# Four small moves in a conformer kernel: queries sooner, pending work earlier, copies before a table load, inputs before weights

## The chip, the core and the metric

The kernel runs on one core of one Trainium2 chip. The metric is the device time of one execution in microseconds; for a kernel I quote the median of its executions. "Changed kernel" is the one with all four moves. Span is the time from the first to the last instruction in a profiled execution; it is some 4 us shorter than the device time. The changed kernel and all experiments gave correct results.

## The reference, cut to what matters

```
B, T, D = 2, 4000, 512; F = 2048; K = 3
h = layernorm(x);  x1 = x + 0.5 * silu(h @ w_ff1_a) @ w_ff1_b      # first feed-forward part
h = layernorm(x1); q, k, v = h @ w_q, h @ w_k, h @ w_v
x2 = x1 + softmax(q @ k.T * D**-0.5) @ v @ w_o                      # attention, each batch by itself
h = layernorm(x2) @ w_pw1; h = h[..., :D] * sigmoid(h[..., D:])     # convolution part
h = depthwise conv of 3 taps; normalised over all tokens per channel
x3 = x2 + silu(h) @ w_pw2
x4 = x3 + 0.5 * silu(layernorm(x3) @ w_ff2_a) @ w_ff2_b             # second feed-forward part
return layernorm(x4)
```

All inputs are bf16.

## The kernel before

The 8000 tokens are worked in 16 chunks of up to 508, a chunk in four tiles of 127 rows. TensorE is never meant to stop: every engine gets its instructions in one fixed order, and the order on TensorE mixes work of several stages, so that a group of matmuls whose inputs are late has others in front of it. Weights of queries and keys are folded into one matrix M, so keys are the normalised tokens themselves.

Attention issues, for each of 32 key tiles of a chunk, four matmuls of scores, an exponential on ScalarE, a running sum on VectorE, and then the four matmuls of values of four steps before (they are put on a list of pending work, `lags`). The next chunk's queries are made on the way, in four groups of four matmuls:

```
for g in range(NCK):                                  # 16 chunks
    for kt in range(KT):                              # 32 key tiles
        ...  # scores -> ps; ACT: exp; DVE: acc += P
        def values(...):                              # 4 matmuls into Yb[0..3]
            ...
            if kt == KT - 1: self.finish_queries(g, done)   # copies Yb away: 2 on ACT, 2 on DVE
        self.lags.append(values)
        ...  # pop one pending piece
        if g + 1 < NCK and 7 <= kt < 7 + TPC:
            self.fetch_queries(...)                   # DMA transposes of keys into lnT[slot]
        if g + 1 < NCK and kt in (14, 16, 18, 20):
            self.q_group(..., (kt - 14) // 2)         # 4 matmuls, copy by ACT (even) or DVE (odd)
        ...  # from chunk 1 on: convolution work of earlier chunks as filler
```

In front of it, the first queries:

```
for dc in range(DC):                # DC = 4
    self.q_group(0, 0, dc)
...
self.attention(old, ...)            # old = 2 pieces of the feed-forward part still pending
```

At the end of the convolution part, for the last two chunks, depthwise sums sit in four PSUM banks (Yb) in turn, get statistics from VectorE, and are copied to SBUF by ScalarE. The `act(self.nr1, ...)` is there only to make ScalarE load the table of Silu early:

```
def finish(cc, between=None):
    for t in (last, tail):
        f, copy = self.depthwise(t, cc)   # 3 matmuls into the next Y bank
        f()                               # DVE: statistics
        copies.append(copy)               # ACT: copy out of the bank, to be issued later
        if t == last and between: between()
    self.conv_scale(cc)                   # DVE aggregate, POOL power
...
for jj in range(DC):
    self.conv_b(last, jj)                 # matmuls, ACT: sigmoid
    if jj == DC - 1:
        self.act(self.nr1, self.onef, AF.Silu, ...)
    copy_away()                           # issues all waiting copies
    self.conv_a(last, jj)
    ...
self.swish(0, 0); self.swish(0, 1); copy_away()
...
def between():
    self.conv_shift(DC - 2)               # DVE, needs POOL's power
    self.swish(0, 2)                      # ACT, needs that shift
finish(DC - 1, between)
self.conv_shift(DC - 1); self.swish(0, 3)
```

And the start. Each x tile comes in two transfers, of 112 and 15 rows:

```
for ti in range(TPC):
    self.load_rows(self.XT[ti], ..., ("SP", "ACT" if ti < 2 else "SP"))
for k in range(2):
    self.load_wa(i["w_ff1_a"], k, "ACT")            # 256 KB each
for k in range(self.NWA): ...                       # the other weights, by SP
...
def head(self):
    self.warm(13)                                   # matmuls on zeros
    ...
    for ti in self.ln_tiles(0, 0, None, ("DVE",) * TPC, lag=1):   # layernorm of 4 tiles
        self.transpose_pe(ti, ...)                  # TensorE, copy by ACT (last: DVE)
        if ti: blocks(ti - 1)                       # 16 matmuls, two 256 KB loads as weights
    blocks(TPC - 1)
```

Of the kernel before, what the change touches and what calls it, by code (L numbers as in the profile page):

```python
# [16 lines left out]
TPC = 4  # L17
CHUNK = TPC * TILE
N = B * T
TCB = -(-T // CHUNK)  # L20
NCK = B * TCB
# [6 lines left out]
DC = D // 128  # L28
# [7 lines left out]
def width(c):  # L36

    return CHUNK if c % TCB < TCB - 1 else T - (TCB - 1) * CHUNK
# [214 lines left out]
class Conformer:  # L253
# [604 lines left out]
                                           reads=b_o[lo:hi], writes=[Buf("out")]))  # L858


    def q_group(self, b, qc, dc):

        s, sl = qc % 2, 1 if b or qc else 0
        ps, b_ps = self.sbank()
        W = width(qc)
        out = ps[:, 0:W].rearrange("p (t k) -> p t k", t=TPC)
        lo = self.query_at(qc, 0)[1]
        for cc in range(DC):
            self.mm(out, self.M[:, cc, dc * 128:(dc + 1) * 128], self.lnT[sl][:, :, cc, lo:lo + W // TPC],
                    cc == 0, cc == DC - 1, [self.b_M] + self.b_lnT[sl], b_ps)  # L870
        if dc % 2:
            self.S.op("DVE", lambda e: e.tensor_copy(self.qT[s][:, dc, 0:W], ps[:, 0:W]),  # L872
                      reads=[b_ps], writes=[self.b_qT[s][dc]])
        else:
            self.act(self.qT[s][:, dc, 0:W], ps[:, 0:W], AF.Copy, [b_ps], [self.b_qT[s][dc]])
# [6 lines left out]
        return qc * CHUNK + ti * n - lo, lo  # L882

    def fetch_queries(self, b, qc, ti):
        sl = 1 if b or qc else 0
        src, rd = self.keys_at(b, self.query_at(qc, ti)[0])
        self.transpose(self.lnT[sl][:, ti], src, rd, [self.b_lnT[sl][ti]])

# [35 lines left out]
    def attention(self, old, hook, done):  # L924
        S = self.S
        LAG = 4
        for g in range(NCK):
            b, qc = divmod(g, TCB)
            s, W = qc % 2, width(g)
            if self.any_score:  # L930
                if qc == 0:
                    self.pop(len(self.lags))
                    if b:
                        for kt in range(KT):
                            self.key_tile(1, kt)
                self.row_max(qc)
            for kt in range(KT):
                kc, kj = divmod(kt, TPC)
                ps, b_ps = self.sbank()
                p = self.nxt("Pa", self.NP - 1) if self.any_score else self.nxt("P", self.NP)  # L940
                for cc in range(DC):
                    self.mm(ps[:, 0:W], self.hT[kc][:, kj, cc, :], self.qT[s][:, cc, 0:W],
                            cc == 0, cc == DC - 1 and not self.any_score,
                            [self.b_hT[kc][kj], self.b_qT[s][cc]], b_ps)
                if self.any_score:
                    self.mm(ps[:, 0:W], self.one3, self.m3[:, 0:W], False, True,
                            [self.b_one3] + self.b_m3, b_ps)
                self.act(self.P[p][:, 0:W], ps[:, 0:W], AF.Exp, [b_ps], [self.b_P[p]], scale=SCALE)
                if kt == 0:
                    S.op("DVE", lambda e, p=p: e.tensor_copy(self.acc[s][:, 0:W], self.P[p][:, 0:W]),  # L950
                         reads=[self.b_P[p]], writes=[self.b_acc[s]])
                else:
                    n = REST if kt == KT - 1 else 128
                    acc = self.acc[s][0:n, 0:W]
                    S.op("DVE", lambda e, p=p, n=n, acc=acc: e.tensor_tensor(  # L955
                        out=acc, in0=acc, in1=self.P[p][0:n, 0:W], op=ALU.add),
                        reads=[self.b_P[p], self.b_acc[s]], writes=[self.b_acc[s]])

                if kt == KT - 1:
                    self.split_sums(g)  # L960
                    if g < NCK - 1:
                        self.sums_by_query(s)

                def values(kt=kt, p=p, g=g, W=W):
                    for dc in range(DC):

                        r = slice(dc * REST, (dc + 1) * REST) if kt == KT - 1 else slice(0, 128)
                        self.mm(self.Yb[dc][:, 0:W], self.h[kt][r, dc * 128:(dc + 1) * 128], self.P[p][r, 0:W],
                                kt == 0, kt == KT - 1, [self.b_h[kt], self.b_P[p]], self.b_Y[dc],
                                inc=kt == KT - 1 or dc == DC - 1,  # L970
                                **({"tile_position": (dc * REST, 0)} if kt == KT - 1 else {}))
                    if kt == KT - 1:
                        self.finish_queries(g, done)

                self.lags.append(values)
                if g == 0 and kt < LAG:
                    self.pop({0: old // 2, 1: old - old // 2}.get(kt, 0))
                elif len(self.lags) > LAG:
                    self.pop(1)
                if g + 1 < NCK and 7 <= kt < 7 + TPC:  # L980
                    self.fetch_queries((g + 1) // TCB, (g + 1) % TCB, kt - 7)
                if g + 1 < NCK and kt in (14, 16, 18, 20):
                    self.q_group((g + 1) // TCB, (g + 1) % TCB, (kt - 14) // 2)
                if not self.any_score and TCB - 1 <= g <= TCB:

                    at = (g - TCB + 1) * KT + kt
                    for k in range(KT):
                        if 6 + k * (2 * KT - 12) // KT == at:
                            self.key_tile(1, k)
                hook(g, kt)  # L990
                self.tick()
# [350 lines left out]
    def program(self, any_score):  # L1342
        i = self.i
# [6 lines left out]
        for ti in range(TPC):  # L1350
            self.load_rows(self.XT[ti], self.x_flat[ti * TILE:(ti + 1) * TILE, :], [self.bx[ti]],
                           ("SP", "ACT" if ti < 2 else "SP"))
        for k in range(2):
            self.load_wa(i["w_ff1_a"], k, "ACT")
        for k in range(self.NWA):
            if k > 1:
                self.load_wa(i["w_ff1_a"], k, "SP")
# [35 lines left out]
        old = 0  # L1393
        for c in range(NCK):
            ff1(c, old)
            old = len(self.lags)
        for dc in range(DC):
            self.q_group(0, 0, dc)

        tail = NCK - 2  # L1400
# [74 lines left out]
        copies = []  # L1475

        def finish(cc, between=None):
            for t in (last, tail):
                f, copy = self.depthwise(t, cc)
                f()  # L1480
                copies.append(copy)
                if t == last and between:
                    between()
            self.conv_scale(cc)

        def copy_away():
            while copies:
                copies.pop(0)()

        self.halo_left(last, 0)  # L1490
        for jj in range(DC):
            self.conv_b(last, jj)
            if jj == DC - 1:
                self.act(self.nr1, self.onef, AF.Silu, [self.b_onef], [self.b_nr1])
            copy_away()
            self.conv_a(last, jj)
            if jj > 1:
                self.conv_shift(jj - 2)
            if 0 < jj < DC - 1:
                self.halo_left(last, jj + 1)  # L1500
            if jj:
                finish(jj - 1)
            else:
                self.halo_left(last, 1)
                f, copy = self.depthwise(tail - 1, DC - 1)
                f()
                copies.append(copy)
# [129 lines left out]
```

## Time and profile before

| | |
|---|---|
| Device time, 3 runs | 2042.21 us (2041.98 to 2042.29) |
| Span of the profiled run | 2037.6 us |
| TensorE busy | 2028.8 us |
| Granted TensorE clock | 0.999 |

TensorE is the bound from the start to the end, and the gain of any move that keeps its work is a stall that goes. A stall shows best as a distance between starts of consecutive matmuls: a line of the timeline reads start, duration (both in us), engine, source line, operation, output<-inputs, shape and count, and in brackets the idle time before it with what ended it.

### The profile page before, as it was taken

How to read it: one execution, taken by the hardware profiler on the slowest of the kernel's cores; microseconds unless marked ns; L12 is line 12 of the kernel's file. 1: busy time of each engine (PE TensorE's matmuls, PEld its weight loads, DVE VectorE, ACT ScalarE, POOL GpSimd, SP SyncE). 2: the span in 40 equal slices, each digit the busy share in tenths (PEclk: the TensorE clock that was granted, in tenths of full speed). 3: DMA queues.
4: the chain of work that ended last, by engine and by line, in shares of the span. 5: the costliest groups of instructions: out<-in, count | busy, mean ns of one | idle time of the engine just before them, and what ended most of it. 6: DMA issues, size and time to landing. Idle time of an engine off the chain costs nothing.

```text
span 2037.6 us, 24579 instructions
## 1 busy us (share of the span) xinstructions
PE 2028.8 (100%) x9682; PEld 1030.0 (51%) x9682; DVE 1081.6 (53%) x2187; ACT 743.6 (36%) x1277; POOL 107.6 (5%) x235
## 2 busy tenths in 40 slices
PE   9999999999999999999999999999999999999999
PEld 5555555554444444445444444444455555555555
DVE  4234443334556667666766676667674444434434
ACT  3433333333333333333333333333345443443433
POOL 1000000000000000000000000000011000000000
PEclk9999999999999999999999999999999999999999
DMA  8122245420101111114421111111243111111111
GB/s 189 49 62 62 54 101 124 96 70 8 27 16 26 26 32 26 26 24 94 108 58 23 26 27 34 23 27 26 44 135 93 32 32 42 32 32 42 26 37 38
DMA packets 253121, 104.42 MB, mean 51 GB/s; under 512 B 193412, under 2 KB 252487, under 8 KB 252999
## 3 DMA queue, kind: packets, MB, share of 16 engines
q1 hardware_dynamic: 251793, 102.18, 21.6%
q8 instruction: 78, 1.28, 0.3%
q10 hardware_dynamic: 1206, 0.60, 0.1%
q14 instruction: 44, 0.36, 0.1%
HBM read 33.77 MB, written 23.34 MB: 28 GB/s over the span
## 4 chain that ended last, share of the span: by engine, by line
PE 98%; ACT 1%; DVE 0%; DMA 0%; SPq 0%; issue 0%; ACTq 0%
PE s L512 56%; PE y L512 42%; ACT work L562 0%; DMA xt<-in_x_dram 0%; ACT keys L562 0%; SPq L574 0%; PE y L540 0%; DVE work L559 0%; ACT L562 0%; PE y L527 0%; DVE work L872 0%; DVE work L955 0%; DVE wff L1208 0%; DVE wff L1095 0%; ACT wff L562 0%
## 5 line engine op out<-in xcount | busy, mean ns | idle before, releaser
L562 ACT ACTIVATE work<-s 128x508 bf16<-128x508 f32 (+3 forms) x1060 | 621.6, 587 | 1212.6 <-PE s L512 1208.1
L512 PE MATMUL s<-work,wff 128*128 128x508 bf16 (+4 forms) x2640 | 628.3, 369 | 0.6 <-DVE work L559 0.2
L512 PE MATMUL s<-work,keys 128*128 128x508 bf16 (+1 forms) x2048 | 516.8, 374 | 0.1
L512 PE MATMUL y<-work,keys 128*128 128x508 bf16 (+2 forms) x2048 | 504.2, 373 | 0.4 <-DVE work L559 0.4
L512 PE MATMUL y<-wff,work 128*127 128x512 bf16 (+1 forms) x2000 | 501.4, 378 | 0.0
L955 DVE TENSOR_TENSOR work<-work 128x508 f32<-128x508 f32 (+2 forms) x496 | 334.4, 674 | 283.1 <-ACT work L562 282.1
L512 PEld LDWEIGHTS s<-work,wff 128*128 128x128 bf16 x2640 | 252.5, 98 | 276.9 <-issue 4.7
L512 PEld LDWEIGHTS y<-wff,work 128*127 128x127 bf16 x2000 | 274.4, 137 | 170.8
L512 PEld LDWEIGHTS s<-work,keys 128*128 128x128 bf16 x2048 | 199.5, 98 | 231.9 <-issue 0.6
L512 PEld LDWEIGHTS y<-work,keys 128*128 128x128 bf16 (+1 forms) x2048 | 193.5, 97 | 234.0 <-issue 6.2
L758 DVE SCALAR_TENSOR_TENSOR xt<-y,xt 127x512 bf16<-127x512 f32 x125 | 77.7, 683 | 364.6 <-PE y L512 364.6
L624 DVE BATCH_NORM_STATS2 work<-xt 127x6 f32<-127x512 bf16 x311 | 195.3, 676 | 4.9 <-DMA xt<-in_x_dram 4.8
L512 PE MATMUL s<-work 128*127 128x512 bf16 (+4 forms) x775 | 195.8, 377 | 1.2 <-DVE work L1326 1.2
L631 POOL TENSOR_TENSOR work<-work 127x4 f32<-127x4 f32 (+1 forms) x76 | 76.5, 1007 | 1128.1 <-DVE work L629 1128.1
L512 PEld LDWEIGHTS s<-work 128*127 128x127 bf16 (+2 forms) x775 | 94.7, 124 | 74.9 <-issue 2.7
L644 DVE TENSOR_SCALAR work<-xt,work 127x512 bf16<-127x512 bf16 x309 | 111.5, 406 | 27.2 <-POOL work L631 23.2
L758 DVE SCALAR_TENSOR_TENSOR xt<-s,xt 127x512 bf16<-127x512 f32 x55 | 38.0, 691 | 148.7 <-PE s L512 148.7
L758 DVE SCALAR_TENSOR_TENSOR xt<-s,work,xt 127x512 bf16<-127x512 f32 x64 | 48.0, 750 | 30.9 <-PE s L512 30.3
L1106 DVE SCALAR_TENSOR_TENSOR wff<-wff,s 128x508 bf16<-128x508 f32 (+1 forms) x57 | 38.7, 679 | 41.7 <-PE s L512 41.5
L562 ACT ACTIVATE wff<-s 128x508 f32<-128x508 f32 (+1 forms) x67 | 39.5, 591 | 54.9 <-PE s L512 54.9
L562 ACT ACTIVATE work<-keys,work 128x508 bf16<-128x508 bf16 (+1 forms) x68 | 52.2, 775 | 0.1
L1187 POOL COPY wff<-wff 128x1 bf16<-128x1 bf16 x56 | 10.4, 187 | 638.1 <-DVE wff L1106 635.3
(92 smaller groups left out, 412.8 us busy)
## 6 DMA issues: line engine op xcount, KB each, us to landing
keys<-keysd SPq DMA_DIRECT2D x62, 128.0 KB, 2.3
keysd<-work SPq DMA_DIRECT2D x14, 448.0 KB, 3.2
out_dram<-work SPq DMA_DIRECT2D x14, 448.0 KB, 3.2
dcvd<-wff SPq DMA_DIRECT2D x48, 127.0 KB, 1.9
keys<-dcvd SPq DMA_DIRECT2D x12, 508.0 KB, 4.9
xt<-in_x_dram SPq DMA_DIRECT2D x13, 448.0 KB, 4.8
wff<-in_w_ff_a_dram SPq DMA_DIRECT2D x14, 256.0 KB, 5.7
work<-work SPq DMA_TRANSPOSE x208, 2.5
```

The lines of the kernel that those rows point to most:

```text
L512: self.S.op("PE", lambda e: e.matmul(out, lhsT, rhs, start=start, stop=stop, **kw), reads=reads, writes=[bank], inc=stop if inc is None el ...
L562: return self.S.op("ACT", lambda e: e.activation(out, in_, func, **kw), reads=reads, writes=writes)
L624: self.S.op("DVE", lambda e: e.bn_stats(self.st[sl][:, ti, 0:6], x), reads=[b_x], writes=[self.b_st[sl][ti]])
L631: S.op("POOL", lambda e: e.tensor_tensor(out=self.rs[sl][:, 0:n], in0=self.mv[sl][:, 0:n, 1], in1=self.neghalf[0:TILE, 0:n], op=ALU.pow), ...
L644: self.S.op("DVE", lambda e: e.tensor_scalar(out, x, self.mv[sl][:, ti, 0:1], self.rs[sl][:, ti:ti + 1], ALU.subtract, ALU.mult), reads=[b ...
L758: self.S.op("DVE", lambda e: e.scalar_tensor_tensor(out=self.XT[g][rows], in0=ps[rows], scalar=scalar, in1=self.XT[g][rows], op0=ALU.mult, ...
L955: S.op("DVE", lambda e, p=p, n=n, acc=acc: e.tensor_tensor(out=acc, in0=acc, in1=self.P[p][0:n, 0:W], op=ALU.add), reads=[self.b_P[p], sel ...
L1106: self.S.op("DVE", lambda e: e.scalar_tensor_tensor(out=out, in0=th, scalar=1.0, in1=ps[:, 0:W], op0=ALU.add, op1=ALU.mult), reads=[b_ps, ...
L1187: S.op("POOL", lambda e: e.tensor_copy(self.G[gs][:, jj, 0:1], self.G[gp][:, jj, CHUNK:CHUNK + 1]), reads=[self.b_G[gp][jj]], writes=[self ...
```

## The change

Its intent: fill or shorten four waits. The third chunk's queries are made at steps 3, 4, 14 and 16 of chunk 1 instead of 14 to 20, from the other transpose buffer, which is free then. One pending feed-forward piece goes in front of the last of the first query groups. In the convolution part the copies go ahead of the table load. At the start, the second weight load moves from ScalarE's queue to SyncE's, behind all x tiles.

```
+    def query_slot(b, qc):
+        return 1 if b or qc == 1 or qc > 2 else 0
 ...  # used in q_group and fetch_queries, in place of: 1 if b or qc else 0
-                if g + 1 < NCK and 7 <= kt < 7 + TPC:
+                if g + 1 < NCK and g != 1 and 7 <= kt < 7 + TPC:
                     self.fetch_queries((g + 1) // TCB, (g + 1) % TCB, kt - 7)
-                if g + 1 < NCK and kt in (14, 16, 18, 20):
-                    self.q_group((g + 1) // TCB, (g + 1) % TCB, (kt - 14) // 2)
+                if g == 0 and 24 <= kt < 24 + TPC:
+                    self.fetch_queries(0, 2, kt - 24)
+                if g + 1 < NCK and kt in ((3, 4, 14, 16) if g == 1 else (14, 16, 18, 20)):
+                    self.q_group((g + 1) // TCB, (g + 1) % TCB, (3, 4, 14, 16).index(kt) if g == 1 else (kt - 14) // 2)
 ...
-        for k in range(2):
-            self.load_wa(i["w_ff1_a"], k, "ACT")
+            if ti in (1, 3):                       # inside the loop over the x tiles
+                self.load_wa(i["w_ff1_a"], ti // 2, "ACT" if ti == 1 else "SP")
 ...
         for dc in range(DC):
+            if dc == DC - 1:
+                self.pop(1)
+                old -= 1
             self.q_group(0, 0, dc)
 ...
         for jj in range(DC):
+            if jj == DC - 1:
+                copies.pop(0)()
             self.conv_b(last, jj)
             if jj == DC - 1:
+                copy_away()
                 self.act(self.nr1, self.onef, AF.Silu, [self.b_onef], [self.b_nr1])
```

More of the change, by code (lines that the diff above doesn't have):

```diff
@@ L858, in store_out @@
                                            reads=b_o[lo:hi], writes=[Buf("out")]))
+    @staticmethod
+    def query_slot(b, qc):
+        return 1 if b or qc == 1 or qc > 2 else 0
     def q_group(self, b, qc, dc):
-        s, sl = qc % 2, 1 if b or qc else 0
+        s, sl = qc % 2, self.query_slot(b, qc)
         ps, b_ps = self.sbank()
@@ L884, in fetch_queries @@
     def fetch_queries(self, b, qc, ti):
-        sl = 1 if b or qc else 0
+        sl = self.query_slot(b, qc)
         src, rd = self.keys_at(b, self.query_at(qc, ti)[0])
```

## The prediction

> **What bounds the kernel now.** I read the page first, then the waits of TensorE, then the timeline around every place where consecutive matmuls start further apart than their size explains, and last the chain of waits near the start and in the stretch between attention and the second feed-forward part.
>
> From the page:
> ```profile
> PE 2028.8 (100%) x9682; PEld 1030.0 (51%) x9682; DVE 1081.6 (53%) x2187; ACT 743.6 (36%) x1277; POOL 107.6 (5%) x235
> PE 98%; ACT 1%; DVE 0%; DMA 0%; SPq 0%; issue 0%; ACTq 0%
> ```
> TensorE has work for 2028.8 of 2037.6 us, at a granted clock of 0.999. So 8.8 us is all that counts as idle. The change adds and removes no matmul on the path taken: it can win only stalls. What the waits view lists is smaller still:
> ```profile
> PE s L512 <- DVE work L1326: 1.2, 1, 1.2
> PE y L527 <- DVE work L644: 1.0, 2, 0.8
> PE y L512 <- DVE work L559: 0.4, 1, 0.4
> PE y L512 <- ACT keys L562: 0.2, 1, 0.2
> ```
> The first line is the start of the kernel, which the change doesn't touch. The second lies in the first layernorm (part D), the third at the end of attention chunk 0 (part A), the fourth in the convolution stretch (part C). A modelled end of a matmul hides stalls that are shorter than the pipeline, so below I take starts: groups of four 128x508 matmuls follow each other at 0.86 us, 0.216 us each.
>
> **What the Trainium skill says.** "Perfetto Trace Analysis", section "Tensor Engine Instruction (MATMUL, LD_WEIGHTS)": the end of a matmul in a profile is estimated, not observed. This trace agrees: a group of four lasts 1.02 us in it, yet the next starts after 0.86. "TensorE: Matmul & The Clock Gate", section "Back-to-back issue gap": N / 2.4 + 2.5 ns, so 214 ns for 508 columns; the trace has 216, so nothing is to be had inside a group. "ScalarE: Activation LUTs", section "What ACT_TABLE_LOAD costs": about 1283 ns and a drain of about 1380 ns; the trace has the 1.28 us, and no such drain (17 ns of idle in front of the load in the convolution stretch). "DMA: Bandwidth & Descriptors", section "Issuing engines are not separate DMA queues": transfers issued by different engines run on the same 16 DMA engines and interleave. In the trace the last x tile, issued by SyncE, landed at 7.09 us beside two weight loads issued by ScalarE.
>
> **Part A: the third chunk's queries as filler.** At the end of chunk 0 the timeline reads:
> ```profile
> 515.67 0.39 PE L512 MATMUL y<-work,keys 32*128 32x508 bf16 x4
> 516.00 1.03 PE L512 MATMUL s<-work,keys 128*128 128x508 bf16 x4
> 516.33 1.08 ACT L562 ACTIVATE work<-y 128x508 bf16<-128x508 f32 x2
> 516.46 0.69 DVE L955 TENSOR_TENSOR work<-work 128x508 f32<-128x508 f32 x1 [1.03 <-ACT work L562]
> 516.97 0.39 PE L512 MATMUL y<-work,keys 128*128 128x508 bf16 x1
> 517.07 1.27 DVE L559 CAST work<-y 128x508 bf16<-128x508 f32 x2
> 517.80 0.98 PE L512 MATMUL y<-work,keys 128*128 128x508 bf16 x3 [0.45 <-DVE work L559]
> 518.62 1.02 PE L512 MATMUL s<-work,keys 128*128 128x508 bf16 x4
> ```
> The four sums of values of chunk 0 (y) must be copied out before chunk 1 may write them: two copies on ScalarE, two on VectorE, the last ending at 517.07 + 1.27 = 518.34. From 516.00 to 518.62 TensorE starts 8 matmuls: 2.62 us where 8 x 0.216 = 1.73 would do, so 0.89 us are lost. Later boundaries lose nothing here, because a convolution pair is issued between the scores and the values. Only chunk 1 has no such filler.
>
> The change issues one of the four query groups (0.86 us) at step 3, just ahead of the scores of step 4. Values then start at 516.00 + 0.86 + 0.86 = 517.73 instead of 516.97. The fourth is due at 517.73 + 3 x 0.216 = 518.38; its copy ends at 518.34, and some 0.05 us pass from a copy to a matmul. So about 0.03 of the 0.89 stays: **0.85 us won**. The group at step 4 comes behind the values, so it is no filler; the work itself is only moved from steps 18 and 20. Its inputs are fetched at steps 24 to 27 of chunk 0, more than 8 us early. The buffer is free again at step 16; the layernorm transposes that reuse it start in the before at 545.6 and their pair of matmuls at 556.42. I expect their slack to shrink from some 3 us to some 1 us, not to vanish.
>
> **Part B: pending feed-forward work.** At the start of attention:
> ```profile
> 453.00 1.33 PE L512 MATMUL s<-work,keys 128*128 128x508 bf16 x4
> 453.20 0.69 DVE L872 CAST work<-s 128x508 bf16<-128x508 f32 x1 [1.04 <-PE s L512]
> 454.17 0.81 PE L512 MATMUL y<-wff,work 128*127 128x512 bf16 x3
> ```
> The first scores take 454.17 - 453.00 = 1.17 us for 0.86 us of work. Their fourth matmul needs the fourth query group, whose copy ends at 453.89: 0.3 us lost. The new order of instructions puts the three pending matmuls (0.65 us) in front of the fourth query group, not between it and the scores. The distance from that group through its 0.69 us copy to the scores stays, and so does the stall. **0 us won**; it only moves 0.65 us later, and the matmuls after it start when they did.
>
> **Part C: copies ahead of the table load.** In the convolution stretch a depthwise group waits for a bank that ScalarE frees only after a table load (starts at 1537.53 and 1538.31: 0.35 us lost). The naive gain is that. But the chain of waits does not run through it:
> ```profile
> 1536.33 1.28 ACT L562
> 1537.82 0.91 ACT keys L562 x2
> 1538.73 1.39 ACT work L562 x2
> 1543.42 4.13 ACT work L562 x6
> ```
> It stays on ScalarE to 1547.55. One copy (about 0.45 us) moves to where ScalarE idles for 1.25 us, the other ahead of the load: the first Silus start 0.40 us sooner. The next limit is close, though:
> ```profile
> 1541.51 0.16 DVE L1222 SCALAR_TENSOR_TENSOR work<-work 128x1 f32<-128x1 f32 x1 [0.73 <-POOL work L1217]
> ```
> This is the last channel block's shift, done at 1541.67. The last Silu of the pair at 1540.92 needs it and already waits: that pair takes 1.59 us, the first 1.50. The shift descends from statistics of the last depthwise groups; VectorE waited 0.27 us for their matmuls, but the previous block's shift, which stands between them in its order, needs a GpSimd result of 1539.44 and holds the second one back. So the last shift comes some 0.08 us sooner, the last Silu as well, and with it all of ScalarE's later work. **0.08 us won**; most of the 0.40 becomes a wait of ScalarE.
>
> **Part D: x tiles ahead of weights.**
> ```profile
> 6.50 0.19 DVE L726 BATCH_NORM_AGGREGATE work<-work 127x2 f32<-127x9 f32 x1
> 7.11 0.69 DVE L624 BATCH_NORM_STATS2 work<-xt 127x6 f32<-127x512 bf16 x1 [0.42 <-DMA xt<-in_x_dram]
> 7.72 0.41 DVE work L644
> 8.17 0.40 PE y L527 x4
> ```
> (The last two lines are the chain's.) The fourth x tile lands at 7.09, in competition with 256 KB of weights that are now issued behind it. Those run at some 27 ns for each of 32 packets on an engine, so I estimate the tile 0.9 us sooner, at 6.2. Its statistics then follow the aggregate at about 6.6. The third tile's normalisation, behind them, is next held by GpSimd's power (6.77 + 0.55, and 0.1 to VectorE): 7.42 instead of 7.72. The transposes move from 8.17 to 7.87, the fourth tile's likewise: **0.30 us won**. The weights moved back land at about 7.1 by my estimate (the same bytes are ahead of them as were ahead of the x tile), and the matmuls that need them start near 7.3.
>
> **Sum.** 0.85 + 0 + 0.08 + 0.30 = 1.23 us, from 2042.21 to 2040.98; I say 2040.95.
>
> **Rivals.** (1) Every stall named is won in full: 0.89 + 0.30 + 0.35 + 0.30 = 1.84, giving 2040.4. For it speaks that each part was aimed at a visible stall; against it the dependences in B and C. (2) The weights land late. Each 0.1 us past 7.3 eats as much of D, and from 7.6 on D is nothing or a loss: 2041.3. For it speaks the small margin, against it that the packets ahead are no more than before. (3) The tighter reuse of the query buffer in A stalls the next convolution pair: up to a microsecond lost, 2041.5 to 2042. Against it stands the slack of about 1 us. (4) A's new copy on ScalarE delays the exponentials behind it; values run four steps later, some 7 us, so I expect nothing.
>
> **Range and chances.** The three runs before lie within 0.31 us, and all parts are under 1 us. Rival 1 sets the low end, rivals 2 and 3 in part the high end: 2040.2 to 2041.7. Two per cent is 41 us, over four times all the idle time: within 2% with 0.99.
>
> **What would show it.** A: in the new trace no TensorE wait on the copies of y near 516 us, and the four values starting 0.216 us apart. B: the first scores still take about 1.17 us. C: the depthwise group follows the residual matmuls without a gap, but ScalarE idles about 0.4 us before the last Silu of the pair, and the transposes that follow gain only 0.1 relative to the starts before the stretch. D: statistics of the fourth tile near 6.6, transposes near 7.87. I am wrong if the first scores take 0.86 us, if the stretch in C gains 0.3, or if the matmuls of the first block wait for a weight load.

## The result, and the profile after

The changed kernel took 2041.37 us (4 runs, 2041.11 to 2041.62), beside 2042.25 us before (4 runs, 2041.98 to 2042.35). That is 0.88 us less, within the predicted range of 2040.2 to 2041.7. Ratios here are the mean time of one kernel's runs over that of the other's of the same rounds, so not quite the ratio of the medians quoted; this one is 0.9996, with an interval of 0.9979 to 1.0013.

The page of the changed kernel has TensorE just as full:
```profile
PE 2028.9 (100%) x9682; PEld 1030.5 (51%) x9682; DVE 1081.5 (53%) x2187; ACT 743.7 (37%) x1277; POOL 107.6 (5%) x235
```
Its list of TensorE's waits (engine, what it ran, whom it waited for, us in total, times, longest) lost three entries and got one:
```profile
PE s L512 <- ACT work L562: 0.4, 1, 0.4
PE y L540 <- ACT work L562: 0.2, 1, 0.2
PE s L512 <- DVE work L559: 0.2, 1, 0.2
```
The waits for y's copies (part A), for a bank behind the table load (part C) and for the normalised tile (part D) are gone. New is the first line: 0.4 us of waiting for ScalarE. Which stretch gained what is seen from the start times of the same matmul in both traces, and I read the four places one by one.

**The end of chunk 0 (A)**, timeline of the changed kernel:
```profile
516.03 1.04 PE L512 MATMUL s<-work 128*128 128x508 bf16 x4
516.90 1.02 PE L512 MATMUL s<-work,keys 128*128 128x508 bf16 x4
517.10 1.27 DVE L559 CAST work<-y 128x508 bf16<-128x508 f32 x2
517.77 1.05 PE L512 MATMUL y<-work,keys 128*128 128x508 bf16 x4
```
The query group (first line) stands in front of the scores, the values follow as one unbroken group of four, and the copies (third line) end at 518.37, just as the fourth is due. All later matmuls start 0.855 us sooner against those before this place.

**The first scores (B)**:
```profile
453.68 2.19 PE L512 MATMUL s<-work,keys 128*128 128x508 bf16 x8
453.88 0.69 DVE L876 CAST work<-s 128x508 bf16<-128x508 f32 x1 [1.69 <-PE s L512]
...
455.71 0.81 PE L512 MATMUL y<-wff,work 128*127 128x512 bf16 x3
```
Eight matmuls of scores take 455.71 - 453.68 = 2.03 us where 8 x 0.216 = 1.73 would do. The stall of 0.30 us has moved and is as long as before; the gain of this stretch is 0.00 us.

**The convolution stretch (C)**:
```profile
1539.40 0.80 ACT L562 ACTIVATE work<-keys,work 128x508 bf16<-128x508 bf16 x1
1540.25 0.16 DVE L1229 SCALAR_TENSOR_TENSOR work<-work 128x1 f32<-128x1 f32 x1 [0.73 <-POOL work L1224]
1540.44 0.81 ACT L562 ACTIVATE work<-keys,work 128x508 bf16<-128x508 bf16 x1 [0.25 <-DVE work L1229]
```
The last Silu (third line) now idles 0.25 us for the shift of the second line. From the attention's end to the second feed-forward part 0.14 us are won.

**The start (D)**:
```profile
6.29 0.75 PE L527 MATMUL y<-work 127*128 127x127 bf16 x8
...
7.43 0.41 DVE L644 TENSOR_SCALAR work<-xt,work 127x512 bf16<-127x512 bf16 x1 [0.17 <-POOL work L731]
7.46 1.05 PE L512 MATMUL s<-work,wff 128*128 128x127 bf16 x16 [0.42 <-ACT work L562]
...
8.35 0.39 PE L527 MATMUL y<-work 127*128 127x127 bf16 x4
```
VectorE did what was predicted: the third tile is normalised from 7.43 (the fourth x tile landed at 5.50, sooner than the 6.2 that I had estimated, which changes nothing behind it). But the transposes of the first tile start only at 6.29, against 5.45 before, for the warm-up matmuls lasted longer; the first two tiles' transposes run together, their copies on ScalarE hold back the first block (0.42 us, the new wait), and the third tile's transposes come at 8.35. From here on everything is 0.03 us later than before. So three stretches are as foretold within 0.06 us, and the fourth won nothing.

The two traces also differ in two places that the change doesn't touch: a convolution pair near 961 us waited 0.29 us in the trace before and not after; and the last output transfer landed 2.49 us after issue before, 3.31 after. The repeats below are for these and for the start.

### The profile page after: what moved, and what is told of

The parts are those of the page before. It is cut to its first block, busy times and chain, and to the rows that moved or that the text cites. A ratio compares the mean times of both kernels' runs of the same rounds, so it can differ in the third digit from the quotient of the medians.

```text
span 2037.1 us, 24581 instructions
## 1 busy us (share of the span) xinstructions
PE 2028.9 (100%) x9682; PEld 1030.5 (51%) x9682; DVE 1081.5 (53%) x2187; ACT 743.7 (37%) x1277; POOL 107.6 (5%) x235
## 3 DMA queue, kind: packets, MB, share of 16 engines
q8 instruction: 78, 1.28, 0.3%
## 4 chain that ended last, share of the span: by engine, by line
PE 99%; ACT 0%; DVE 0%; issue 0%; POOL 0%; DVEq 0%
PE s L512 56%; PE y L512 42%; ACT work L562 0%; DVE wff L1215 0%; PE y L540 0%; ACT keys L562 0%; POOL work L1224 0%; DVE work L559 0%; DVE work L876 0%; PE y L527 0%; DVE wff L1102 0%; DVE work L1222 0%; ACT xt L562 0%; DVE work L835 0%; DVE work L1229 0%
```

## The experiments

Twelve kernels, in three lots that each ran on one chip with runs of the kernel before. A single execution scatters by about 1 us either way (that kernel alone: 2041.67 to 2043.69 in the last lot), as much as the whole effect. So the medians decide little, and I compare start times of the same matmul, stretch by stretch: these repeat to some 0.01 us. The table gives by how much the matmuls after a stretch start sooner (-) or later than in the first trace of before, counted from its beginning. "Start" is the start of the first Silu of the first block. All times in us. All outputs are right.

| kernel | median (before) | start | first scores | end of chunk 0 | near 961 | convolution stretch |
|---|---|---|---|---|---|---|
| before, first trace | 2042.25 | 10.98 | 0 | 0 | 0 | 0 |
| changed, first trace | 2041.37 (2042.25) | 11.01 | 0.00 | -0.855 | -0.29 | -0.14 |
| before_again | 2042.22 (2042.56) | 11.41 | 0.00 | 0.00 | +0.15 | +0.01 |
| after_again | 2041.76 (2042.56) | 11.56 | 0.00 | -0.85 | -0.29 | -0.14 |
| a_only | 2042.00 (2042.56) | 11.17 | 0.00 | -0.85 | +0.04 | +0.01 |
| d_only | 2042.18 (2042.56) | 11.52 | 0.00 | 0.00 | -0.11 | +0.01 |
| b_between | 2041.98 (2042.45) | 11.71 | -0.31 | 0.00 | -0.29 | +0.01 |
| c_shift_last | 2041.75 (2042.45) | 11.21 | 0.00 | 0.00 | -0.29 | -0.35 |
| a_late | 2041.90 (2042.45) | 11.21 | 0.00 | +0.01 | -0.29 | +0.02 |
| d_even | 2042.61 (2042.45) | 11.31 | 0.00 | 0.00 | -0.04 | +0.01 |
| best | 2040.71 (2042.53) | 10.93 | -0.31 | -0.85 | -0.24 | -0.34 |
| best_warm10 | 2040.83 (2042.53) | 11.02 | -0.31 | see below | | |
| after_no_d | 2041.18 (2042.53) | 10.99 | 0.00 | -0.85 | -0.29 | -0.14 |
| after_third | 2041.44 (2042.53) | 11.12 | 0.00 | -0.85 | -0.29 | -0.14 |

All verdicts are "same" at 2%. (best_warm10's trace lacks a few matmul records, so matmuls can't be matched by number behind the first scores.)

**before_again**, the kernel before, unchanged.

> The kernel before, unchanged, as a second trace and as the noise floor. Theory: three things in the traces vary from run to run without the change: how long the warm-up matmuls run at 425 ns (to 4.11 us in the first trace of before, to 5.81 in the first of the changed kernel), the 0.29 us wait of a convolution pair near 961 us (there in before, gone in the changed kernel), and the landing of the last output transfer (2.49 us against 3.31 us after issue). Then at least one of the three differs here from the first trace of before, and the ratio is 1.0000 within 0.0002. Rival: they belong to the kernels; then this trace repeats 4.11, 0.29 and 2.49.

The ratio was 0.9998, and all three things came out otherwise: the slow warm-up matmuls lasted to 5.35 us (before: 4.11), the wait near 961 was 0.44 us, and the last transfer landed after 4.01 us. That run took 2043.52 us. So all three vary without the change, and the first trace of before was lucky in the start and the end.

**after_again**, the changed kernel, unchanged.

> The changed kernel, unchanged, as a second trace. Theory: the early transposes start at 7.87 for the third tile if the slow matmuls end near 4 us, and near 8.35 if they last to 5.8 us again; the stall at the end of chunk 0 is gone (0.85 us) and the one in the first scores is there (0.3 us). Median 0.8 to 1.2 us under before. Rival for the start: x tiles ahead of weights itself makes the slow phase longer, then it ends at 5.8 us here too.

Ratio 0.9996. The end of chunk 0 and the first scores repeat exactly. The start was worse than in the first trace: all 13 warm-up matmuls ran slowly, to 6.65 us, and the third tile's transposes came at 8.89. This matches neither of the two times that I gave. The rival (the move itself prolongs the slow phase) isn't needed for this, though a small effect of the move can't be excluded: over the 13 traces with 13 warm-up matmuls, 7 to 11 of them are slow with the loads of before (eight traces), and 9 to 13 with the moved load or in d_even (five traces). The ranges overlap, and the kernel before alone covers 7 to 10. "TensorE: Matmul & The Clock Gate", section "What's actually happening", says that the number of cold matmuls varies from run to run, since the window that decides is free-running; these traces agree, with 7 to 13.

**a_only**, the third chunk's queries alone (that part of the diff above).

> Only the third chunk's queries sooner. Theory: it carries most of the gain: the matmuls behind the end of chunk 0 start 0.85 us sooner against those before it, median 0.8 to 0.9 us under before. Rival: part of the gain seen at 961 us in the changed kernel (0.29 us) comes from this part too; then that wait is gone here and the median is 1.1 to 1.2 us under.

The stretch gained 0.85 us, and the wait near 961 was there (0.33 us), so the rival falls. The median was 0.56 us under before, less than expected: its trace has a slower end (3.75 us to the last landing), and the scatter is larger than the difference. What decides is the stretch.

**d_only**, the loads alone (that part of the diff above).

> Only x tiles ahead of weights. Theory: normalisation of the third tile starts at 7.43 instead of 7.72 in any case; TensorE gains the 0.30 us only where the slow matmuls end near 4 us, and about nothing where they end near 5.8 us. The median is then 0 to 0.3 us under before. Rival: the late weight load (7.76 us in the first trace of the changed kernel) is what held TensorE, then the first block's matmuls show a wait for a DMA in their middle, and nothing is gained at either clock.

Nothing was won, and the rival's sign is there:
```profile
7.09 0.61 PE L512 MATMUL s<-work,wff 128*128 128x127 bf16 x8
...
8.40 0.62 PE L512 MATMUL s<-work,wff 128*128 128x127 bf16 x8 [0.70 <-DMA wff<-in_w_ff_a_dram]
```
Here the warm-up ended early enough (first transposes at 5.93), TensorE reached the first block at 7.09, and its second half stood still for the moved weight load, which landed at 8.35. In the four traces with the move it landed at 7.76, 7.95, 8.04 and 8.35; in the eight with the loads and the warm-up of before, at 6.72 to 7.63. A likely reason is seen in the stretches of the start, 4.50 to 5.50 us (columns: stretch, length, busy time of PE, PEld, DVE, ACT and POOL, clock, DMA share, GB/s), in the first trace of before:
```profile
4.50:5.00 0.50, 0.50 (x4) 0.20 (x2) 0.31 (x2) 0.00 (x0) 0.30 (x1) 1.00 0.97 295
5.00:5.50 0.50, 0.50 (x4) 0.21 (x3) 0.47 (x3) 0.00 (x0) 0.00 (x0) 1.00 1.14 362
```
and of the changed kernel:
```profile
4.50:5.00 0.50, 0.50 (x3) 0.19 (x2) 0.32 (x2) 0.00 (x0) 0.30 (x1) 1.00 0.60 150
5.00:5.50 0.50, 0.50 (x3) 0.23 (x2) 0.43 (x2) 0.00 (x0) 0.00 (x0) 1.00 0.64 184
```
The DMA engines run at 0.60 and 0.64 instead of 0.97 and 1.14. The x tiles are nearly through, and the load behind them was issued only at 3.48 us, after six others of SyncE at 0.46 us each, where ScalarE had issued it at 2.25.

**d_even**, all x tiles ahead of both weight loads, the second of these issued sooner.

```
-                ("SP", "ACT" if ti < 2 else "SP"))
+                ("SP", "ACT"))                     # all 15-row parts by ACT
         for k in range(2):
-            self.load_wa(i["w_ff1_a"], k, "ACT")
+            self.load_wa(i["w_ff1_a"], k, ("ACT", "SP")[k])
```

> All x tiles ahead of all weights, with the 15-row parts issued by ScalarE and the 112-row parts by SyncE, so that the second weight load is issued at about 2.65 us instead of 3.48. Theory: in the change that load landed late (7.8 to 8.4 us against 6.9 to 7.3) because it was issued 1.2 us later, after six other issues of SyncE. Here it lands near 7.2, the fourth x tile before 6, normalisation of the third tile starts at 7.43, and no matmul of the first block waits for weights; TensorE gains up to 0.3 us where its warm-up ends early, and less where not. Rival: one ring shared by x and weights is slower than two whatever the time of issue; then the second load lands near 8 us again.

The second load was issued at 2.59 and landed at 7.26, the fourth x tile at 5.06, and the third tile's normalisation started at 7.44: as expected. But now the first load was the last to land, at 7.70, and the first block waited 0.69 us for it (first matmul at 7.75, first Silu at 11.31). My "no matmul of the first block waits for weights" was wrong, and the rival was wrong about which load is late. So late issue fits the late landing of the moved load, but isn't shown alone, since the other load moved back too. The four x tiles and two weight loads, 1 MB, are all down at 7.0 to 7.8 us with the loads of before, at 7.7 here and at 7.8 to 8.4 with the move: no order tried made that sooner, and the order decides which is last.

**b_between**, the pending matmuls behind the fourth query group, nothing else.

```
         for dc in range(DC):
             self.q_group(0, 0, dc)
+        self.pop(1)
+        old -= 1
```

> The pending feed-forward matmuls behind the fourth query group instead of in front of it, nothing else of the change. Theory: the stall of the first scores comes from the copy of the fourth query group, so 0.65 us of other matmuls between the two hide it: the first scores take 0.86 us instead of 1.17, and every later matmul starts 0.30 us sooner. Rival: the stall has another cause (the exponential's table load, or the place of the scores), then it stays at 0.3 us here too.

```profile
453.73 0.81 PE L512 MATMUL y<-wff,work 128*127 128x512 bf16 x3
454.38 1.88 PE L512 MATMUL s<-work,keys 128*128 128x508 bf16 x8
456.10 0.81 PE L512 MATMUL y<-wff,work 128*127 128x512 bf16 x3
```
Eight matmuls of scores in 456.10 - 454.38 = 1.72 us: no stall, 0.31 us won, as expected. So the copy of the fourth group was the cause, and one place further back in the order makes the whole difference.

**c_shift_last**, the copies ahead of the table load alone, with the third shift behind the statistics of both last groups.

```
-                if t == last and between:
+                if t == tail and between:
                     between()
```

> The copies ahead of the table load alone, and the shift of the third channel block behind the statistics of both last depthwise groups. Theory: the last Silu of that pair waits for a chain of VectorE and GpSimd, in which the third shift's wait for GpSimd holds back the last statistics; with it out of the way they come about 0.25 us sooner. The stretch from the start of the last convolution block to the second feed-forward part then gains 0.3 to 0.4 us against before, where the change as made gained 0.14. Rival: ScalarE alone limits, then the gain is 0.14 again; or the shift, now later, delays the Silu of the third block and nothing or a loss comes.

VectorE's timeline there, of this kernel:
```profile
1538.69 1.40 DVE L1208 BATCH_NORM_STATS2 wff<-y 128x6 f32<-128x444 f32 x2
1540.00 0.14 DVE L1222 SCALAR_TENSOR_TENSOR work<-work 128x1 f32<-128x1 f32 x1
1540.12 0.25 DVE L1215 BATCH_NORM_AGGREGATE work<-wff 128x2 f32<-128x21 f32 x1
1541.11 0.16 DVE L1222 SCALAR_TENSOR_TENSOR work<-work 128x1 f32<-128x1 f32 x1 [0.73 <-POOL work L1217]
```
Both statistics run through, the third shift (second line) no longer stands between them, and the last shift comes sooner. 0.35 us were won, against 0.14 of the change as made. The chain of VectorE and GpSimd, and not ScalarE alone, held the rest back. (The later shift without the copies wasn't run.)

**a_late**, as a_only, with the first two groups at steps 4 and 6.

```
# against a_only, both lines cut
-                ... kt in ((3, 4, 14, 16) if g == 1 ...
+                ... kt in ((4, 6, 14, 16) if g == 1 ...
```

> The third chunk's queries sooner, with groups at steps 4, 6, 14 and 16, so that the first comes behind the values of step 4 and not in front of them. Theory: only the group ahead of those values fills the wait for the copies, so the stall is back (values 0.83 us apart at their start, 0.87 us lost in all) and nothing is gained. Rival: the earlier fetch, or the moved load on ScalarE and VectorE, was part of the gain, then some of the 0.85 us stays.

```profile
517.20 0.39 PE L512 MATMUL y<-work,keys 128*128 128x508 bf16 x1
518.03 0.98 PE L512 MATMUL y<-work,keys 128*128 128x508 bf16 x3 [0.45 <-DVE work L559]
```
The first value matmul stands 0.83 us ahead of the others again, and the stretch gains nothing (0.01 us later). The same fetches, the same groups, the first one step later and the second two, and all of the 0.85 us is gone: it is the place ahead of the values that counts.

**best**, A as made, B as in b_between, C as in c_shift_last, loads as before.

> Queries sooner as in the change, feed-forward matmuls behind the fourth query group, copies ahead of the table load with the third shift behind the last statistics; loads as in before. Theory: the four stretches add up, 0.85 + 0.31 + 0.35 = 1.5 us from the end of the first block's start to the last matmuls, so about 1.5 us under before in the median, give or take 0.4 of scatter, and 0.5 us under the changed kernel. Rival: the gains overlap somewhere (a stall that is hidden by another), then the stretches sum to less.

Median 2040.71 us beside 2042.53, ratio 0.9990 (0.9977 to 1.0004): 1.82 us less, and 0.73 less than the changed kernel of the same lot. The three stretches gained 0.31, 0.85 and 0.34, in sum 1.50 us, so nothing overlaps. (The rest of the 1.82 is not theirs: in this trace 0.24 us is the place near 961, and the medians scatter.) It is the fastest kernel, though still within 2% of both others.

**best_warm10**, the same with 10 warm-up matmuls in place of 13.

> The same with 10 warm-up matmuls instead of 13. Theory: where the slow clock lasts, the 13 warm-up matmuls end at 5.8 to 6.6 us and hold back the first transposes, whose data is ready at 5.4; with 10 they end by 5.4 in any case, and up to 0.5 us is won in the start. Rival: TensorE, less busy early, gets its full clock later, the first transposes and blocks run at the slow rate, and the start is the same or longer.

The first transposes did start at 5.40, and yet the first Silu came at 11.02, no sooner; the median was 2040.83. Neither theory holds: the full clock came no later (last slow matmul at 4.96 us), but the fourth x tile landed at 7.12, and in all nine traces with the loads of before the first Silu follows that landing by 3.89 to 3.95 us, whatever the warm-up did.

**after_no_d**, the changed kernel with the loads of before.

> The changed kernel with the loads of before. Theory: x tiles ahead of weights is worth nothing on average, because the same bytes must land before the first block is done; the second weight load lands near 7.2 instead of 8, the fourth x tile near 7.3 instead of 6.2, and the median is that of the changed kernel within 0.3 us. Rival: it was worth its 0.3 us in most executions, and the traces happened to be unlucky; then this kernel is 0.3 us slower than the changed one.

Median 2041.18, 0.26 under the changed kernel of the same lot; the x tile landed at 7.10, the second load at 6.88. So x tiles ahead of weights won nothing that these runs can show.

**after_third**, the changed kernel once more.

> The changed kernel again, on the same chip as the three others, for the comparison: 0.8 to 1.0 us under before.

Median 1.09 us under before, a little more than expected. In its three comparisons (the first result, and two of the lots) the changed kernel was 0.88, 0.80 and 1.09 us under before.

## Why the prediction was right, and where it was not

**The bound: right.** The change moved only stalls, and the time stayed within 2%. One citation needs its context: the formula that the prediction takes from "Back-to-back issue gap" stands there for a matmul by itself, and the same section puts a stream of matmuls with 512 columns at about 131 ns each. The traces don't show that: a stream of 508 columns runs at 216 ns each, and the measurement decides.

**A: right, to 0.01 us.** 0.85 was predicted; 0.85 was measured in all six traces that have it and whose matmuls can be matched. The mechanism (one group between the scores and the values covers the copies) is shown by a_late. The tighter reuse of the query buffer (rival 3) brought no wait in any trace, nor did A's new copy on ScalarE (rival 4): the matmuls keep their 0.85 us up to the next place that changes, near 961 us.

**B: right, 0.** The distance from the fourth query group to the scores is what counts; b_between shows it from the other side, with 0.31 us won.

**C: mechanism right, size off by 0.06 us.** The mis-sized term is "the last shift comes some 0.08 us sooner". It came 0.14 sooner. In the changed kernel the third shift waits for GpSimd with VectorE idle, and the next statistics start 0.10 us after it; in the trace before, that distance was 0.17. I had kept the 0.17. The lines, first of before, then of the changed kernel:
```profile
1539.62 0.14 DVE L1222 SCALAR_TENSOR_TENSOR work<-work 128x1 f32<-128x1 f32 x1
1539.79 0.70 DVE L1208 BATCH_NORM_STATS2 wff<-y 128x6 f32<-128x508 f32 x1
```
```profile
1538.43 0.16 DVE L1229 SCALAR_TENSOR_TENSOR work<-work 128x1 f32<-128x1 f32 x1 [0.19 <-POOL work L1224]
1538.54 0.69 DVE L1215 BATCH_NORM_STATS2 wff<-y 128x6 f32<-128x508 f32 x1
```
My "ScalarE idles about 0.4 us before the last Silu" was 0.25, in part for the same reason. The rest is how it is counted: Silus that nothing delays start 0.70 us apart here and last 0.80, so 0.10 of a delay hides behind the Silu before. Between starts the delay is 1540.44 - 1539.40 - 0.70 = 0.34 us. No run has C as made alone, but A, B and D by themselves left this stretch as it was (0.02 us at most), so the 0.14 is C's.

**D: wrong, 0.30 predicted, nothing won.** The part about VectorE held: the third tile was normalised from 7.43 us (foretold: 7.42). The step that failed is "The weights moved back land at about 7.1 by my estimate (the same bytes are ahead of them as were ahead of the x tile)". The runs put them at 7.76 to 8.35. I had counted bytes and left out the time of issue: 1.2 us later, so that the DMA engines were busy at only 0.60 and 0.64 from 4.5 to 5.5 us. (That this is why the load is late is argued from these shares and from d_even; that it is late is shown, and in d_only that it holds up the first block.) The other half of the error is a hidden assumption: that TensorE starts its first transposes at 5.45, as in the one trace I had. In the twelve other traces with 13 warm-up matmuls it was 5.87 to 6.65. With the x tile out of the way the start is bound by that, or by the weights: in the first trace of the changed kernel by the warm-up and ScalarE's copies, in d_only by the weights. Rival 2 described the second of these, with too small a chance, and its sign, a wait of the first block for a weight load, came in d_only and in none of the three traces of the changed kernel. Nor would the early start of the first trace of before have saved D, by an estimate from the traces: there the second half of the first block started at 7.33; with a load at 7.76, the earliest seen, it ends at 7.76 + 8 x 0.056 = 8.21, and the third tile's transposes behind it were at 8.17 without the move. The four starts with the move average 11.30 us (first Silu), the eight without it and with the same warm-up 11.20; the difference is within their scatter (10.93 to 11.71).

**The sum.** A and C, as the traces show them, are 0.99 us, and the medians of the three comparisons give 0.80 to 1.09. The prediction's 1.23 is that plus the 0.30 of D less the 0.06 of C. So the time fell into the range with one of the four mechanisms wrong, since the range was 1.5 us wide: the sum is no proof of its parts, and the stretches are.

**What stays open.** The wait near 961 us. A convolution pair waits there for the last of four DMA transposes. In both traces of before it was 0.29 and 0.44 us, in all three of the changed kernel 0, but also 0 in three kernels with only one part each, and a_only has it while a_late, which differs in nothing near it, has not. So the change as such need not be its cause. In each trace SyncE stops for up to 2 us shortly before, while one instruction fetch of 16 KB is in the DMA engines; that fetch took 1.49 us or more in the five traces with waits of 0.18 us and above, and less in the others. That they belong together is argued from this order alone; no run takes the fetch away.

## What to carry to other kernels

When an engine is full, find its stalls as distances between starts, and put a filler exactly between the instruction that produces late data and the one that waits for it: one place too early or too late, the same work hides nothing. A wait that goes is only worth what the next wait in the chain lets through, so look for the second limit before counting the first. And where the start of a kernel depends on the landing of several loads, moving one ahead moves another behind; count when each can be issued, not only its bytes, and take more than one trace before a few tenths of a microsecond are believed.

## What the Trainium skill lacked or had wrong

- "ScalarE: Activation LUTs", section "What ACT_TABLE_LOAD costs": of the roughly 1380 ns drain that the page adds to every table load, the traces show nothing. In the convolution stretch the load of 1.28 us starts 17 to 19 ns after the instruction before it, and ScalarE goes on 11 ns after it.
- "TensorE: Matmul & The Clock Gate", section "What's actually happening": the page's warm-up budget of about 3.4 us and its variation of 500 ns are too tight for this kernel. With TensorE busy without a break from 1.18 us on, the slow warm-up matmuls lasted to between 4.11 and 6.65 us, that is 2.9 to 5.5 us; its counts of 6 to 14 cold matmuls do fit (7 to 13).
- No page that I read has a figure for how much the landing of one and the same transfer varies between executions, or for what an instruction fetch beside it costs. Here the last output transfer landed 2.49 to 4.05 us after issue in kernels whose ends are the same (2.49 and 4.01 in two traces of one kernel), with a 16 KB fetch of 0.95 to 1.78 us near it in each trace; whether that is the cause is open.
